# Retention and mixture of experts on one core: the second expert's rows prepared at later steps, weight splits moved into its pass, and one ordering between transfers dropped

## The chip, the cores and the metric

One core of a Trainium2 chip runs the whole kernel. Its engines are TensorE (PE, with its weight loads PEld), VectorE (DVE), ScalarE (ACT), GpSimd (POOL) and SyncE (SP, which only issues transfers here). The metric is device time in microseconds of one execution, given as the median of the runs shown. The granted clock of TensorE is a share of full speed: 1.0 is 2.4 GHz, 0.5 is 1.2 GHz.

## The reference, cut to what matters

```python
# attention with a decaying state, for each batch and head
for t in range(S):                                   # S = 768, head_dim 64, 8 heads, 4 batches
    state = gamma * state + outer(k[t], v[t])
    y[t] = scale * (q[t] @ state)
x = y as rows                                        # 3072 rows of 512
# one expert of 8 per row
e_idx = argmax(x @ w_gate, axis=1)
gate_w = softmax(x @ w_gate) at e_idx ;  eom = sigmoid(x @ w_output_gate)
for e in range(8):
    mask = e_idx == e
    h = maximum(x[mask] @ w1[e], 0)                  # 512 -> 1024
    out[mask] = gate_w * eom * (h @ w2[e])           # 1024 -> 512
```

## The kernel before, in words

The first part (to about 145 us) is the attention, in chunks; it also routes each row and scatters it by GpSimd into `srt`, a table in HBM that has 448 slots for each expert. Rows of empty slots are filled by three scatters of `zrow` (line L636): one with the indices `fi` for the first expert, two with the indices `si` for the rest. Nothing may read a slot before all of this is written; `after(ld.ins, sent)` says so for a load.

The second part multiplies the rows with the weights. Numbers are float32 split in a high and a low part, so each product is three matmuls: high by high, high by low, low by high. Experts are taken in an order of rank. The first expert is cut in two: its first 224 slots (`head`) run while the routing still ends; its last 224 (`left_load`, `left_turn`, `left_cast`, `left_sub`; tiles `xp`, `pt`, `ph`, `pw`) are pass e = 0 of the main loop. The seven other experts are passes 1 to 7, with 436 down to 364 slots.

The main loop runs over steps `s`, eight in a pass (`f` = 0 to 7), one for each block of 128 hidden units:

- `stage1(s)`: 12 matmuls (L1221) into one of three PSUM banks (`st`, and two named `h`), then `hh` on ScalarE (L1226, ReLU and rounding) and `hl` on VectorE (L1227, the rest).
- `stage2(s-1)`: 12 matmuls (L1241) that take `hh` and `hl` of the step before and add to the four accumulators `a`. At the end of a pass VectorE turns the accumulators (`ot`, L1247).
- `load_x(e)` loads the rows of an expert from `srt` (tile `xl`, four transfers on SyncE, L1188). That of pass 1 waits for all scatters.
- `prep_x(e, dc)` prepares one quarter of these rows: a transposition on VectorE (`xt`, L1207), a rounding on ScalarE (`xh`, L1208), a difference on VectorE (`xw`, L1209). The first quarter also takes the row numbers (`idi`, L1202), which is the first instruction that waits for `xl`.
- `load_weights(s)` loads a block of both weight matrices into one of three buffers `raw` (L158 and L162); `split_weights(s)` makes its high parts on ScalarE (`whi`, L184 and L186) and its low parts on VectorE (`wlo`, L191 and L193). The table in the `while split` line says how far the splits stay back at each step.

Each engine takes its instructions in the order in which they are written here; only SyncE's order in the second part is set by a scheduler. So an instruction of VectorE or ScalarE that waits holds up all that is written behind it. Block numbers below are values of `s`: block 10 is the third block of pass 1.

Of the kernel before, what the change touches and what calls it, by code (L numbers as in the profile page):

```python
# [32 lines left out]
def retention_moe_kernel(  # L33
# [17 lines left out]
    E, DM, DF = w1.shape  # L51
# [5 lines left out]
    NF = DF // P  # L57
# [10 lines left out]
    srt = dpool.tile([DROWS, ROW], F32, name="srt")  # L68
# [95 lines left out]
    def load_weights(s: int):  # L164
        for _ in weight_parts(s):
            pass
# [29 lines left out]
    def split_weights(s: int):  # L196
        for part in range(2):
            split_hi(s, part)
        for part in range(2):
            split_lo(s, part)  # L200
# [10 lines left out]
    def behind(later, earlier):  # L211
        tc.add_manual_dep(later, earlier.name, mybir.DependencyInfo(
            mybir.DependencyClass.Sync, mybir.DependencyReason.DATA), reason="one send at a time")
# [6 lines left out]
    with ExitStack() as actx:  # L220
# [28 lines left out]
        def after(ins, others):  # L249
            for o in others:  # L250
                tc.add_manual_dep(ins, o.name, mybir.DependencyInfo(
                    mybir.DependencyClass.Sync, mybir.DependencyReason.DATA), reason="sorted rows complete")
# [522 lines left out]
        def emit_head(n):  # L775
            return send(out.rearrange("t (a x) -> (t a) x", a=4), hd["idx"][:, n:n + 1], hd["ot"][:, n], 4 * NT)
# [171 lines left out]
        def left_load(eng, part):  # L948
            if part == 0:
                hd["p"] = wpool.tile([P, 8 * SEG], F32, name="xp", tag="raw", bufs=3)[:, 0:NL * SEG].rearrange("p (n x) -> p n x", x=SEG)  # L950
            t = hd["p"]
            for a in range(2 * part, 2 * part + 2):
                ld = eng.dma_start(
                    t[32 * a:32 * a + 32],
                    srt[ds(rank_e[0] * SLOTS + HEAD, LEFT), a * SEG:(a + 1) * SEG].rearrange("(n i) x -> i n x", i=32))
                if a % 2 == 0:
                    after(ld.ins, sent)

# [19 lines left out]
        def left_ids():  # L978
            hd["pm"] = hpool.tile([P, NL], I32, name="pm0")
            nc.vector.tensor_copy(hd["pm"], hd["p"][:, :, P])  # L980
            nc.vector.tensor_tensor(out=hd["pm"], in0=hd["pm"], in1=slot, op=ALU.max)
            return hd["pm"]
# [167 lines left out]
    with ExitStack() as mctx:  # L1150
# [26 lines left out]
        NS = E * NF  # L1177
# [5 lines left out]
        def load_x(e):  # L1183
            r0, n = PASS[e]
            nb = math.ceil(n / 32)
            t = mp.tile([P, NB, SEG], F32, name="xl", tag="xl")
            for a in range(4):
                ld = nc.sync.dma_start(  # L1188
                    t[32 * a:32 * a + 32, 0:nb],
                    srt[ds(r0, 32 * nb), a * SEG:(a + 1) * SEG].rearrange("(n i) x -> i n x", i=32))  # L1190
                if e == 1 and a == 0:
                    after(ld.ins, sent)
            xr[e] = t
# [17 lines left out]
        def stage1(s):  # L1211
            e, f = divmod(s, NF)
            hi, lo = wts[s]
            xh, xl = xs[e]
            C = PASS[e][1]
            ps = next_bank()
            n = 0
            first_of = (hi, xh), (lo, xh), (hi, xl)
            for dc, (l, r) in ([(dc, lr) for g in (0, 2) for lr in first_of for dc in (g, g + 1)] if e == 0
                               else [(dc, lr) for dc in range(NDC) for lr in ((hi, xh), (hi, xl), (lo, xh))]):  # L1220
                nc.tensor.matmul(ps[:, 0:C], l[:, 0, dc * P:dc * P + P], r[dc][:, 0:C] if e == 0 else r[:, dc, 0:C],  # L1221
                                 start=(n == 0), stop=(n == 3 * NDC - 1))
                n += 1
            hh = mp.tile([P, CAPS[0]], F32R, name="hh", tag="hh", bufs=3)[:, 0:C]
            hl = mp.tile([P, CAPS[0]], F32R, name="hl", tag="hl", bufs=3)[:, 0:C]
            relu = nc.scalar.activation(hh, ps[:, 0:C], AF.Relu)  # L1226
            nc.vector.scalar_tensor_tensor(out=hl, in0=ps[:, 0:C], scalar=0.0, in1=hh.bitcast(F32),  # L1227
                                           op0=ALU.max, op1=ALU.subtract)
            hs[s] = (hh, hl)
            return relu.ins  # L1230

        def stage2(s):
            e, f = divmod(s, NF)
            hi, lo = wts.pop(s)
            hh, hl = hs.pop(s)
            C = PASS[e][1]
            nb = math.ceil(C / 32)
            for d in range(4):
                w = slice(d * P, d * P + P)
                for n, (l, r) in enumerate(((hi, hh), (hi, hl), (lo, hh))):  # L1240
                    mm = nc.tensor.matmul(accs[d][:, 0:C], l[:, 1, w], r, start=(f == 0 and n == 0),  # L1241
                                          stop=(f == NF - 1 and n == 2))
            if f == NF - 1:

                ot = mp.tile([P, NB, P], F32, name="ot", tag="ot", bufs=2)
                for d in range(4):
                    nc.vector.transpose(ot[:, 0:nb, d * 32:d * 32 + 32],  # L1247
                                        accs[d][:, 0:32 * nb].rearrange("p (n i) -> p n i", i=32))
                ots[e] = ot
            return mm.ins  # L1250

        def emit(e, n):
            return send(out.rearrange("t (a x) -> (t a) x", a=4), xs["m", e][:, n:n + 1], ots[e][:, n], 4 * NT)

        def stage2_last(f, tb):
            hi, lo = wts[(E - 1) * NF + f]
            hh, hl = hs[(E - 1) * NF + f]
            w = slice(tb * P, min(tb * P + P, CAPS[-1]))
            n = w.stop - w.start
            for x, (l, r) in enumerate(((hh, hi), (hl, hi), (hh, lo))):  # L1260
                mm = nc.tensor.matmul(rows_of[tb][0:n], l[:, w], r[:, 1], start=(f == 0 and x == 0),
                                      stop=(f == NF - 1 and x == 2))
            return mm.ins

        def emit_last(tb):
            n = min(P, CAPS[-1] - tb * P)
            orow = mp.tile([P, DM], F32, name="orow", tag="orow", bufs=NTB)
            (nc.vector.tensor_copy if tb % 2 else nc.scalar.copy)(orow[0:n], rows_of[tb][0:n])
            send(out, idl[0:n, tb:tb + 1], orow[0:n], NT)
# [9 lines left out]
        loaded, split = NF + 2, NF  # L1279
        for s in range(NS + 1):  # L1280
            e, f = divmod(s, NF)
            if s == 1:
                load_x(1)
            while loaded < min(NS, s + NF + 1):
                load_weights(loaded)
                loaded += 1
            if f == 2 and 0 < e < E - 1:
                load_x(e + 1)
            if s < NS:
                relu = stage1(s)  # L1290
            if 1 <= s <= NS - NF:
                done = stage2(s - 1)
            elif s == NS:
                for tb in range(NTB):
                    stage2_last(NF - 2, tb)
                    stage2_last(NF - 1, tb)
                    emit_last(tb)
            elif s > 0 and s != NS - 2:
                for x in range(f - 1 if s < NS - 1 else NF - 3, min(f, NF - 2)):
                    for tb in range(NTB):  # L1300
                        done = stage2_last(x, tb)
            if s == 1:
                xs["m", 0] = left_ids()
            elif s == NF + 2:
                odd_rows()
            f0 = 3 if e == 0 else 4
            if f0 <= f < (f0 + 4 if e == 0 else 7) and e + 1 < E:
                for dc in (f - f0,) if e == 0 or f < 6 else (2, 3):
                    prep_x(e + 1, dc)
            while split < min(NS, s + NF - {3: 1, 4: 2, 5: 3, 6: 3, 7: 3, 8: 2, 9: 1}.get(s, 0)):  # L1310
                split_weights(split)
                split += 1
            if e >= 1 and s < NS and f >= 1:
                for n in range(2 * f - 2, min(math.ceil(PASS[e - 1][1] / 32), 2 * f)):
                    behind(emit(e - 1, n), done if n % 2 else relu)
            if e == 0:
                if f < HEAD // 32:
                    behind(emit_head(f), relu)
            if s == NS - NF:
                idl = load_idl(E - 1)  # L1320
# [4 lines left out]
    with tc.If(odd > 0):  # L1325
        with ExitStack() as octx:
# [72 lines left out]
            for r in range(1, E):  # L1399
                nov = nc.values_load(over[0:1, r - 1:r], min_val=0, max_val=SLOTS)  # L1400
                with tc.If(nov > 0):
                    e = nc.values_load(order[0:1, r - 1:r], engines=(mybir.EngineType.SP,), min_val=0, max_val=E - 1)
# [47 lines left out]
```

## Time and profile before

| | |
|---|---|
| median of 3 runs | 446.66 us (446.25 to 447.26) |
| the profiled execution, its own time | 444.65 us |
| its span in the trace | 442.9 us |
| TensorE busy | 409.9 us, 93% of the span |
| VectorE, ScalarE, GpSimd busy | 264.9, 199.3, 150.2 us |

The execution's own time is 1.75 us longer than its span: what lies before the first and behind the last instruction. A busy TensorE is not TensorE at its peak, since matmuls overlap and their ends are modelled; the start of a matmul is the safer number, and the text goes by starts.

### The profile page before, as it was taken

How to read it: one execution, taken by the hardware profiler on the slowest of the kernel's cores; microseconds unless marked ns; L12 is line 12 of the kernel's file. 1: busy time of each engine (PE TensorE's matmuls, PEld its weight loads, DVE VectorE, ACT ScalarE, POOL GpSimd, SP SyncE). 2: the span in 40 equal slices, each digit the busy share in tenths (PEclk: the TensorE clock that was granted, in tenths of full speed). 3: DMA queues.
4: the chain of work that ended last, by engine and by line, in shares of the span. 5: the costliest groups of instructions: out<-in, count | busy, mean ns of one | idle time of the engine just before them, and what ended most of it. 6: DMA issues, size and time to landing. Idle time of an engine off the chain costs nothing.

```text
span 442.9 us, 13007 instructions
## 1 busy us (share of the span) xinstructions
PE 409.9 (93%) x5080; PEld 389.5 (88%) x5082; DVE 264.9 (60%) x712; ACT 199.3 (45%) x411; POOL 150.2 (34%) x213
## 2 busy tenths in 40 slices
PE   7798998987989999799999999999999999999991
PEld 3677888976879898799999999999999999999881
DVE  2526777975887873576674565566466477475110
ACT  3334575773784822354443443353443354453110
POOL 7444022221223613213004443441542442441532
PEclk9989899998999999699999999999999999999997
DMA  9999999895551648359628437646745944940002
GB/s 181 206 222 231 212 268 221 211 262 161 172 141 54 233 140 198 119 172 255 211 95 210 159 126 178 180 125 188 211 125 158 231 139 151 228 142 14 30 26 72
DMA packets 125624, 73.74 MB, mean 166 GB/s; under 512 B 55845, under 2 KB 114105, under 8 KB 125552
## 3 DMA queue, kind: packets, MB, share of 16 engines
q1 hardware_dynamic: 119200, 59.07, 52.2%
q0 software_dynamic: 5872, 13.50, 9.2%
q8 instruction: 42, 0.69, 0.7%
q10 hardware_dynamic: 480, 0.23, 0.2%
q14 instruction: 30, 0.25, 0.2%
HBM read 59.63 MB, written 13.90 MB: 166 GB/s over the span
## 4 chain that ended last, share of the span: by engine, by line
PE 49%; issue 6%; POOL 3%; DMA 3%; DVE 1%; SPq 1%; POOLq 0%; ACT 0%; DVEq 0%
PE a L1241 24%; PE h L1221 17%; PE st L1221 8%; POOL out_dram L203 3%; DMA srt<-zrow,si 1%; DMA xl<-srt 1%; SPq L1188 1%; DVE pt L963 0%; POOLq L203 0%; DVE xw L1209 0%; ACT xh L1208 0%; DVE xt L1207 0%; POOLq L1135 0%; DVE hl L1227 0%; POOLq L1324 0%
## 5 line engine op out<-in xcount | busy, mean ns | idle before, releaser
L203 POOL DMA_INDIRECT out_dram<-ot,idi x77 | 78.6, 1021 | 138.9 <-ACT hh L1226 113.5
L1241 PE MATMUL a<-hh,whi 128*128 128x224 f32 (+6 forms) x224 | 75.8, 338 | 3.2 <-ACT hh L1226 3.2
L1241 PE MATMUL a<-hl,whi 128*128 128x224 f32 (+6 forms) x224 | 75.9, 339 | 0.1
L1241 PE MATMUL a<-hh,wlo 128*128 128x224 f32 (+6 forms) x224 | 75.7, 338 | 0.0
L191 DVE TENSOR_TENSOR wlo<-raw,whi 128x512 fp32r<-128x512 f32 x64 | 44.0, 687 | 34.5 <-ACT whi L184 32.9
L184 ACT CAST whi<-raw 128x512 fp32r<-128x512 f32 x64 | 39.5, 617 | 42.3 <-PE a L1241 37.7
L1221 PE MATMUL h<-xh,wlo 128*128 128x408 f32 (+6 forms) x148 | 50.6, 342 | 0.0
L1221 PE MATMUL h<-xw,whi 128*128 128x408 f32 (+6 forms) x148 | 50.6, 342 | 0.0
L1221 PE MATMUL h<-xh,whi 128*128 128x408 f32 (+6 forms) x148 | 50.6, 342 | 0.0
L636 POOL DMA_INDIRECT srt<-row,posi x20 | 20.2, 1012 | 77.5 <-ACT ex L481 11.7
L1241 PEld LDWEIGHTS a<-hh,whi 128*128 128x128 f32 x224 | 42.7, 191 | 3.7 <-ACT hh L1226 3.3
L1227 DVE SCALAR_TENSOR_TENSOR hl<-h,hh 128x224 fp32r<-128x224 f32 (+7 forms) x43 | 23.4, 544 | 37.0 <-ACT hh L1226 37.0
L193 DVE TENSOR_TENSOR wlo<-raw,whi 128x512 fp32r<-128x512 f32 x64 | 43.8, 684 | 0.0
L1241 PEld LDWEIGHTS a<-hl,whi 128*128 128x128 f32 x224 | 42.7, 191 | 0.8 <-DVE hl L1227 0.4
L1241 PEld LDWEIGHTS a<-hh,wlo 128*128 128x128 f32 x224 | 42.8, 191 | 0.4
L1226 ACT ACTIVATE hh<-h 128x224 fp32r<-128x224 f32 (+7 forms) x43 | 20.7, 481 | 49.8 <-PE h L1221 49.8
L368 PE MATMUL st<-vs,kn 64*64 64x64 f32 x704 | 34.4, 231 | 7.6 <-issue 3.9
L186 ACT CAST whi<-raw 128x512 fp32r<-128x512 f32 x64 | 39.4, 616 | 0.2
L368 PEld LDWEIGHTS st<-vs,kn 64*64 64x64 f32 x704 | 27.9, 141 | 6.9 <-ACT sx L428 2.2
L1208 ACT CAST xh<-xt 128x416 fp32r<-128x416 f32 (+2 forms) x28 | 14.9, 533 | 40.4 <-DVE xt L1207 40.4
L428 ACT COPY sx<-st 128x256 f32<-128x256 f32 x44 | 16.4, 373 | 32.9 <-PE st L368 31.7
L1221 PEld LDWEIGHTS h<-xh,whi 128*128 128x128 f32 x148 | 27.8, 188 | 0.4
(259 smaller groups left out, 889.6 us busy)
## 6 DMA issues: line engine op xcount, KB each, us to landing
raw<-in_moe_w_dram SPq DMA_DIRECT2D x128, 256.0 KB, 3.4
kn<-in_k_dram SPq DMA_DIRECT2D x24, 256.0 KB, 5.7
vn<-in_v_dram SPq DMA_DIRECT2D x24, 256.0 KB, 5.5
qn<-in_q_dram SPq DMA_DIRECT2D x14, 256.0 KB, 4.8
qn<-in_q_dram SPq DMA_DIRECT2D x5, 512.0 KB, 6.5
xl<-srt SPq DMA_DIRECT2D x12, 211.2 KB, 5.7
xl<-srt SPq DMA_DIRECT2D x12, 195.0 KB, 5.4
out_dram<-ot,idi POOLq DMA_INDIRECT x77, 3.0
```

Of the source, the lines that this page charges most:

```text
L184: nc.scalar.copy(hi[:, 0], raw[:, 0])
L186: nc.scalar.copy(perm(wts[s][0], s), plain(raw, s))
L191: eng.tensor_sub(lo[:, 0], raw[:, 0], hi[:, 0].bitcast(F32))
L193: eng.tensor_sub(perm(lo, s), plain(raw, s), perm(hi, s).bitcast(F32))
L203: st = nc.gpsimd.indirect_dma_start(out=dst, out_offset=bass.IndirectOffsetOnAxis(ap=idx, axis=0), in_=src, in_offset=None, bounds_check=n ...
L368: mm = nc.tensor.matmul(o, l, m, start=s, stop=True, skip_group_check=True)
L428: ins = nc.scalar.copy(t, st).ins
L636: ins = nc.gpsimd.indirect_dma_start(out=srt, out_offset=bass.IndirectOffsetOnAxis(ap=idx, axis=0), in_=src, in_offset=None, bounds_check= ...
L1221: nc.tensor.matmul(ps[:, 0:C], l[:, 0, dc * P:dc * P + P], r[dc][:, 0:C] if e == 0 else r[:, dc, 0:C], start=(n == 0), stop=(n == 3 * NDC ...
L1226: relu = nc.scalar.activation(hh, ps[:, 0:C], AF.Relu)
L1227: nc.vector.scalar_tensor_tensor(out=hl, in0=ps[:, 0:C], scalar=0.0, in1=hh.bitcast(F32), op0=ALU.max, op1=ALU.subtract)
L1241: mm = nc.tensor.matmul(accs[d][:, 0:C], l[:, 1, w], r, start=(f == 0 and n == 0), stop=(f == NF - 1 and n == 2))
```

## The change

Three edits, all around pass 0 and the first steps of pass 1:

- The four quarters of the second expert's rows, `prep_x(1, 0)` to `prep_x(1, 3)`, stood at steps 3, 4, 5 and 6. They now stand at step 5 (quarter 0), step 6 (quarters 1 and 2) and step 7 (quarter 3). For later passes the rule stays as it was.
- The table of splits holds back more at steps 6 to 10: blocks 10 and 11, which were split at steps 6 and 7, are split at step 8 with block 12; up to step 11 each step has its splits one block later.
- The load of the first expert's second half (`left_load`) joins the group of transfers on `srt` that need no order among themselves, so that the scatters of `zrow` into the other experts' empty slots no longer wait for it.

```diff
@@ left_load
                     srt[ds(rank_e[0] * SLOTS + HEAD, LEFT), a * SEG:(a + 1) * SEG].rearrange("(n i) x -> i n x", i=32))
+                tc.add_to_no_dep_group("srt", ld.ins)
                 if a % 2 == 0:
                     after(ld.ins, sent)
@@ main loop, step s = 8 * e + f
-            f0 = 3 if e == 0 else 4
-            if f0 <= f < (f0 + 4 if e == 0 else 7) and e + 1 < E:
-                for dc in (f - f0,) if e == 0 or f < 6 else (2, 3):
+            if (5 if e == 0 else 4) <= f < (8 if e == 0 else 7) and e + 1 < E:
+                for dc in ((0,), (1, 2), (3,))[f - 5] if e == 0 else (f - 4,) if f < 6 else (2, 3):
                     prep_x(e + 1, dc)
-            while split < min(NS, s + NF - {3: 1, 4: 2, 5: 3, 6: 3, 7: 3, 8: 2, 9: 1}.get(s, 0)):
+            while split < min(NS, s + NF - {3: 1, 4: 2, 5: 3, 6: 4, 7: 5, 8: 3, 9: 2, 10: 1}.get(s, 0)):
                 split_weights(split)
                 split += 1
```

On VectorE, in pass 0 from the `hl` of step 3 to the first `hl` of pass 1 (`hl<-st,hh 128x436`, step 8), the order before is:

```order
L1227 SCALAR_TENSOR_TENSOR hl<-h_3108,hh 128x224
L1202 CAST idi<-xl 128x14
L1207 STREAM_TRANSPOSE xt<-xl 128x448
L1209 TENSOR_TENSOR xw<-xt,xh 128x448
L1227 SCALAR_TENSOR_TENSOR hl<-h_3153,hh 128x224
...
L1227 SCALAR_TENSOR_TENSOR hl<-st,hh 128x224
...
L1227 SCALAR_TENSOR_TENSOR hl<-h_3108,hh 128x224
...
L191 TENSOR_TENSOR wlo<-raw,whi 128x512
L193 TENSOR_TENSOR wlo<-raw,whi 128x4x4x32
L1227 SCALAR_TENSOR_TENSOR hl<-h_3153,hh 128x224
```

and of the change, where lines between L957 and L1306 are numbered one higher:

```order
L1228 SCALAR_TENSOR_TENSOR hl<-h_3153,hh 128x224
L1228 SCALAR_TENSOR_TENSOR hl<-st,hh 128x224
L1203 CAST idi<-xl 128x14
L1208 STREAM_TRANSPOSE xt<-xl 128x448
L1210 TENSOR_TENSOR xw<-xt,xh 128x448
L1228 SCALAR_TENSOR_TENSOR hl<-h_3108,hh 128x224
...
L1228 SCALAR_TENSOR_TENSOR hl<-h_3153,hh 128x224
L1208 STREAM_TRANSPOSE xt<-xl 128x448
L1210 TENSOR_TENSOR xw<-xt,xh 128x448
L1228 SCALAR_TENSOR_TENSOR hl<-st,hh 128x436
```

The `hl` of steps 4 (`h_3153`) and 5 (`st`) moved ahead of `idi`; two quarters stand between the `hl` of steps 6 and 7, and the last one stands between those of steps 7 and 8. No split is left among them: those of blocks 10, 11 and 12 now follow the four `ot` behind the `hl` of step 8. ScalarE's `hh` and `xh` moved in the same way.

On GpSimd, the last scatter of rows (`bposi`), the two scatters of `zrow` by `si`, and the read of `n_pad`, by which it branches past further such scatters, before (the names in brackets are counters: DMAHW of SyncE's and ScalarE's transfers, DMASW of GpSimd's, the others of engines):

```order
L636 DMA srt<-row,bposi 6784x520 [waits Activation_49]
L636 DMA srt<-zrow,si 6784x520 [waits DMAHW6_49,DMAHW5_49,DMAHW7_49,DMAHW0_49,DVE_49]
L636 DMA srt<-zrow,si 6784x520 [waits DMASW3_49,DVE_49]
L1135 TENSOR_LOAD n_pad [waits DVE_49]
L1135 ISA x2
L1136 COMPARE_AND_BRANCH
```

and of the change:

```order
L636 DMA srt<-row,bposi 6784x520 [waits Activation_49]
L636 DMA srt<-zrow,si 6784x520 [waits DVE_49]
L636 DMA srt<-zrow,si 6784x520 [waits DMASW3_49,DVE_49]
L1136 TENSOR_LOAD n_pad [waits DVE_49]
L1136 ISA x2
L1137 COMPARE_AND_BRANCH
```

The first scatter lost its four waits for the transfers of `left_load` and keeps the one for its indices; the rest stands as it stood.

On SyncE, behind the weights of block 17, the rows of the change read as follows; before, the read of `n_odd` (a count that VectorE makes at step 10) stood four blocks of weights behind the `xl` of pass 2:

```order
L1324 TENSOR_LOAD n_odd
L1324 ISA x2
L158 ISA
L158 DMA raw<-in_moe_w_dram 128x4x128
L162 ISA
L162 DMA raw<-in_moe_w_dram 128x512
L1189 ISA
L1189 DMA xl<-srt 32x13x130
```

So the weights of block 18 and the rows of pass 2 now stand behind a wait for VectorE's `n_odd`.

## Rows read from the trace of the kernel before

**Rows 1.** The page: granted clock in 40 slices, in tenths.

```profile
PEclk9989899998999999699999999999999999999997
```

**Rows 2.** Timeline of TensorE, steps 3 to 10: start, length, engine, line, operation, [idle before].

```profile
169.25 0.39 PE L1221 MATMUL h<-ph,whi 128*128 128x224 f32 x2
...
174.62 0.39 PE L1221 MATMUL st<-ph,whi 128*128 128x224 f32 x2
...
179.27 0.55 PE L1241 MATMUL a<-hh,whi 128*128 128x224 f32 x1 [3.16 <-ACT hh L1226]
...
188.97 0.37 PE L1221 MATMUL st<-xh,whi 128*128 128x436 f32 x1
...
190.75 0.35 PE L1221 MATMUL st<-xh,whi 128*128 128x436 f32 x1
...
192.67 0.37 PE L1221 MATMUL h<-xh,whi 128*128 128x436 f32 x1
...
197.43 0.36 PE L1221 MATMUL h<-xh,whi 128*128 128x436 f32 x1
```

**Rows 3.** Windows: stretch, length, busy of five engines, PEclk, DMA share, GB/s.

```profile
176.12:179.27 3.15, 0.00 (x0) 0.00 (x0) 1.00 (x3) 0.82 (x2) 0.00 (x0) 0.80 1.11 362
179.27:184.96 5.69, 5.54 (x25) 5.27 (x25) 3.31 (x7) 1.39 (x3) 1.94 (x2) 0.51 0.27 89
```

**Rows 4.** The chain that ended last, 155 to 190 us: start, length, what.

```profile
162.71 6.15 DMA srt<-zrow,si
...
171.81 5.64 DMA xl<-srt
```

**Rows 5.** Timeline of VectorE, 158 to 212 us.

```profile
158.42 0.16 DVE L1125 TENSOR_TENSOR si<-sl,pidx 128x1 int32<-128x1 f32 x1
...
171.21 0.38 DVE L1227 SCALAR_TENSOR_TENSOR hl<-h,hh 128x224 fp32r<-128x224 f32 x1
177.64 0.18 DVE L1202 CAST idi<-xl 128x14 int32<-128x14 f32 x1 [6.05 <-DMA xl<-srt]
177.72 0.64 DVE L1207 STREAM_TRANSPOSE xt<-xl 128x448 f32<-128x448 f32 x1
178.99 0.62 DVE L1209 TENSOR_TENSOR xw<-xt,xh 128x448 fp32r<-128x448 f32 x1 [0.63 <-ACT xh L1208]
179.54 0.38 DVE L1227 SCALAR_TENSOR_TENSOR hl<-h,hh 128x224 fp32r<-128x224 f32 x1
179.84 0.64 DVE L1207 STREAM_TRANSPOSE xt<-xl 128x448 f32<-128x448 f32 x1
...
211.48 0.17 DVE L1202 CAST idi<-xl 128x13 int32<-128x13 f32 x1 [0.77 <-DMA xl<-srt]
```

**Rows 6.** Timeline of ScalarE, 170 to 179 us.

```profile
170.79 0.36 ACT L1226 ACTIVATE hh<-h 128x224 fp32r<-128x224 f32 x1 [0.31 <-PE h L1221]
178.40 0.56 ACT L1208 CAST xh<-xt 128x448 fp32r<-128x448 f32 x1 [7.25 <-DVE xt L1207]
178.87 0.35 ACT L1226 ACTIVATE hh<-h 128x224 fp32r<-128x224 f32 x1
```

**Rows 7.** Timeline of GpSimd: the first scatter of `zrow` by `si`.

```profile
161.43 0.97 POOL L636 DMA_INDIRECT srt<-zrow,si  x1 [7.30 <-DVEq L1136]
```

**Rows 8.** Timeline of SyncE: the issues of weights of block 9, of `xl` of pass 2.

```profile
163.77 0.52 SPq L162 DMA_DIRECT2D raw<-in_moe_w_dram  x1
...
201.28 2.26 SPq L1188 DMA_DIRECT2D xl<-srt  x4
```

**Rows 9.** Tile `raw`, 188 to 216 us: last line.

```profile
DMA to landing us min/median/max: 2.9/4.5/8.2
```

**Rows 10.** Tile `xl`, 200 to 216 us: last line.

```profile
DMA to landing us min/median/max: 5.4/6.8/8.2
```

**Rows 11.** The page, costliest groups: busy us, mean ns of one | idle before.

```profile
L191 DVE TENSOR_TENSOR wlo<-raw,whi 128x512 fp32r<-128x512 f32 x64 | 44.0, 687 | 34.5 <-ACT whi L184 32.9
...
L1227 DVE SCALAR_TENSOR_TENSOR hl<-h,hh 128x224 fp32r<-128x224 f32 (+7 forms) x43 | 23.4, 544 | 37.0 <-ACT hh L1226 37.0
```

## The prediction

> **What bounds it now.** I read the page first. TensorE is busy for nearly all of the second part, and among its slices of granted clock one stands out after the attention: a 6 in a row of nines, around 180 us [rows 1]. The timeline of TensorE there shows why. Step 5 of pass 0 begins at 174.62, and its `stage2` should follow 12 matmuls later; it begins at 179.27, after 3.16 us idle for `hh` [rows 2]. Behind the wait the matmuls are slow: the windows show the clock at 0.80 in the idle stretch and 0.51 in the next 5.69 us, so nearly all of that stretch is at 1.2 GHz [rows 3].
>
> Then I asked why `hh` of step 4 was late. On ScalarE it stands behind `xh` of the second expert's first quarter, and starts right after it, at 178.87 [rows 6]. `xh` waited 7.25 us for `xt`, and VectorE, which makes `xt`, sat 6.05 us before `idi` until the transfer `xl` landed [rows 5, 6]. The chain of waits carries this further back: `xl` was held by the second scatter of `zrow`, 6.15 us from its start at 162.71 until SyncE was released, and the last of its four transfers took 5.64 us from 171.81, so it landed at 177.45 [rows 4]. So for one quarter of rows that nobody needs before step 8, two engines kept in order hold back what TensorE needs at step 5. From step 8 to the end TensorE runs step after step, so what is saved here should move the end by as much.
>
> **What the wait costs.** Steps of pass 0 with nothing in the way take (174.62 − 169.25) / 2 = 2.685 us [rows 2]. From 174.62 three of them would bring step 8 to 182.68; it begins at 188.97 [rows 2]. The loss is 6.29 us. Two parts make it up: the first matmul of `stage2` comes 3.31 us after 174.62 + 1.34 = 175.96, and the 24 matmuls of the stretch from 179.27 to 184.96 take 5.69 us where 2.685 is the rate at full clock, 3.00 us more [rows 2, 3].
>
> The Trainium skill (TensorE: Matmul & The Clock Gate, Terms) puts the penalty of a lowered clock at the time spent low times (1 − K/N), here a half. The low time, an estimate from the windows, is (1 − 0.80)/0.5 × 3.15 + (1 − 0.51)/0.5 × 5.69 = 6.8 us [rows 3], which by that rule is 3.4 us and would make the loss 6.7. The rows say 3.0, since for the first 1.3 us of the low time TensorE had nothing to run; the sum goes by the rows.
>
> **Edit 1: the rows taken up later.** Nothing is added: four `xt`, `xh` and `xw` move. I follow the new order with durations of before. `hh` starts 170.79 − 169.25 = 1.54 us after its step, and `hl` 0.42 after `hh` [rows 2, 5, 6]. So `hl` of step 5 starts at 174.62 + 1.54 + 0.42 = 176.58 and frees VectorE 0.30 later (179.54 to 179.84 [rows 5]), at 176.88. If `xl` is there, `idi` follows, and no `hh` or `hl` of steps 4 and 5 waits for it: the loss of 6.29 us goes.
>
> What is late next: the quarters. One of them takes VectorE 1.82 us from the start of `xt` to its next instruction (177.72 to 179.54), because `xw` waits for ScalarE [rows 5]. Step 6 begins at 174.62 + 2.685 = 177.30, its `hl` at 179.26, so quarter 1 begins at 179.56, quarter 2 at 181.38, `hl` of step 7 at 183.20 and quarter 3 at 183.50. Its `xh` starts 0.68 later and takes 0.56 [rows 5, 6], so it ends at 184.74; its `xw` starts 1.27 later, takes 0.62 [rows 5], and ends at 185.39. TensorE wants quarter 3 with the tenth matmul of step 8, 190.75 − 188.97 = 1.78 us into it [rows 2], at 182.68 + 1.78 = 184.46. It waits some 0.33 us for `xh`, and one matmul (0.20) later another 0.40 for `xw`: **0.75 us lost**. Quarters 0 to 2 are in time by this reckoning. Bounds: 0 if VectorE and ScalarE run half a step ahead of this, 1.05 if `xl` lands as late as now (next paragraph).
>
> **Edit 3: the scatters no longer held.** The first `si` is ready at 158.42 + 0.16 = 158.58 [rows 5], and the scatter starts at 161.43 [rows 7]. Waiting for VectorE alone, it starts between at once and 0.97 us later (the length of one scatter [rows 7]); so the pair moves forward by 1.9 to 2.85 us. SyncE is free for it: its last issue ahead of `xl` is that of block 9, at 163.77 for 0.52 [rows 8]. With the same 6.15 and 5.64 us behind it, `xl` lands at 174.6 to 175.55, ahead of the 176.88 at which VectorE now asks for it. Beside edit 1 this is worth little: at 177.45 `idi` would start at 177.64 and `xt` at 177.72, against 176.96, which delays `hl` of step 6 from 179.26 to 179.54 [rows 5] and everything behind it by 0.28. **Worth 0.3 us**, already in the 0.75; the lower bound is 0, the upper, with edit 1 undone, the 1.9 to 2.85 us by which `idi` would come earlier.
>
> **Edit 2: splits moved.** The same casts and subtractions are issued, and the splits of blocks 10 and 11 leave the place where they would have stood between the `hl` of steps 6 and 8. Blocks 10, 11 and 12 are split behind `ot` of step 8. Step 8 starts at 182.68, takes 192.67 − 188.97 = 3.70 us and loses 0.75, so step 9 starts at 187.13 and step 10, 197.43 − 192.67 = 4.76 later, at 191.89 [rows 2]. Block 10 is needed at step 10 and ready near 190: no wait. But a `raw` buffer is free only when its block is split, so loads of block 13 on start later against TensorE than before. Step 13 starts at 187.13 + 4 × 4.76 = 206.17 and its `hl` is not yet asked for; step 14's `stage2` asks for it at 206.17 + 4.76 + 2.4 + 0.2 = 213.5. Ahead of it on VectorE stand `idi`, quarter 0 of pass 2 and the split of block 19 (two `wlo` of 0.6 to 0.7 [rows 11]). Now `xl` of pass 2 is issued at 201.28 and `idi` starts at 211.48 [rows 5, 8]. Its issue follows block 18, for which the split of block 15 must be done; by the same reckoning that is near 200.4, so the issue stays where it is while TensorE comes 5.5 us earlier. If the landing stays too, `hl` ends at 211.48 + 1.9 + 1.3 + 0.5 = 215.2 and TensorE waits **1.7 us**. If its transfers land in the 5.4 us of the fastest and not in 6.8 to 8.2 [rows 10], `idi` starts near 209 and the wait is **0**. Fewer weights are queued ahead of it (blocks 16 and 17 are asked for about a microsecond earlier), so I take 0.6, nearer to the fast end. The wait for `n_odd` now ahead of block 18 on SyncE costs nothing: VectorE makes `n_odd` before the split of block 15, for which block 18 waits anyway.
>
> **The sum.** 6.29 − 0.75 − 0.6 = 4.9 us. On its own time the profiled execution would come to 444.65 − 4.9 = 439.7; that execution is 2.0 below the median of the runs, and the same 4.9 off the median gives 441.7.
>
> **The rivals.**
>
> *A, the half clock comes back at step 8.* The waits of 0.33 and 0.40 us are short, and the clock fell here behind one of 3.16 [rows 2, 3]. But other small waits stand close by, and if it falls once more, it costs up to the 3.0 us measured for the 24 matmuls: 441.7 to 444.7, say 443.8. Chance 0.13.
>
> *B, the rows of pass 2 come late.* The `hl` of step 13 is late by the whole 1.7 us, as above: 442.4. If one more step is late by as much, because its weights need the 8.2 us of the slowest load and not the median 4.5 [rows 9], it is 6.29 − 0.75 − 3.4 = 2.1, so 444.5. Chance 0.14.
>
> *C, slower: the three `raw` buffers turn into the bound.* Block 14 is asked for near 191.7; with 8.2 us [rows 9], then its high part (0.6, as a `xh`), its second low part (0.69 [rows 11]) and `hl` of step 10 (0.54 [rows 11]) `stage2` could start at 201.7, against 191.89 + 4.76 + 2.6 = 199.25, some 2.5 us late. Each third block waits for the one before, so blocks 14, 17 and 20 would lose 7.5: 446.66 − 5.5 + 7.5 = 448.7. It decides once the three lose more than 5.5 together. Against it: the median is 4.5, at which block 14 leaves a cushion of more than a microsecond. Chance 0.05.
>
> *D, no change:* the wait of step 5 is for something else and stays, or is given back in full. 446.7. The chain names each link, so 0.06.
>
> **How the numbers follow.** The forecast, 440.4 to 442.8 (both new waits at 0, 440.4; both at their upper ends, 1.05 and 1.7, 443.1), has 0.62. The spread of the runs, 446.25 to 447.26, adds half a microsecond at the low end: 439.8. At the high end the range takes in A and most of B: 444.7. What lies outside is C, D and the rest of B, under 2 in 10. About 0.2% (0.9 us) is what a measurement of this kernel tells from no change: faster 0.88, same 0.07, slower 0.05.
>
> **What would show it.** In the profile of the changed kernel: no wait over 1 us on TensorE between 162 us and its end, no 6 among the slices near 180; the first scatter by `si` at 158.9 to 159.5; `idi` of pass 1 right behind `hl` of step 5, without a wait for `xl`; two short waits near 184.5 at the tenth and eleventh matmul of step 8, and step 9 at 187.1; a wait of 0 to 1.7 us in step 14. It is wrong if the clock is low again between 178 and 190, if `idi` still waits for `xl`, or if ScalarE's `whi` waits for `raw` hold `hh` in steps 10 to 14.

## The result and the profile after

| | before | after |
|---|---|---|
| median of 9 runs each | 446.25 us (443.31 to 447.26) | 440.89 us (438.42 to 443.90) |
| span of the profiled execution | 442.9 us | 439.3 us |
| its first matmul of pass 0 | 162.24 us | 162.50 us |
| from the start of step 5 to that of step 16 | 51.32 us | 47.51 us |

The ratio is 0.9893 (0.9859 to 0.9928): 4.8 us faster, 3.2 to 6.3 by the interval, with 4.9 forecast. Here and below a ratio is taken from the fast runs alone (none over 1.5% above the fastest of its kernel) and a median from all runs, so a ratio is not the quotient of two medians. The two traces differ by 3.6 us in span, and all of it arises between step 5 and step 16 (3.81 us; pass 0 begins 0.26 later, and from step 16 to the end it is 216.99 and 216.92 us).

The page after: span, and the granted clock in 40 slices. The 6 of [rows 1] is gone.

```profile
span 439.3 us, 13006 instructions
PEclk9899899998999999999999999999999999999997
```

TensorE after, as in [rows 2], steps 5, 8, 9, 14 and 15 by their first matmuls, and the matmuls that waited:

```profile
174.87 0.39 PE L1222 MATMUL st<-ph,whi 128*128 128x224 f32 x2
...
182.91 0.37 PE L1222 MATMUL st<-xh,whi 128*128 128x436 f32 x1
...
184.49 0.36 PE L1222 MATMUL st<-xh,wlo 128*128 128x436 f32 x1
185.06 0.47 PE L1222 MATMUL st<-xh,whi 128*128 128x436 f32 x1 [0.21 <-ACT xh L1209]
185.72 0.47 PE L1222 MATMUL st<-xw,whi 128*128 128x436 f32 x1 [0.19 <-DVE xw L1210]
...
187.57 0.37 PE L1222 MATMUL h<-xh,whi 128*128 128x436 f32 x1
...
211.29 0.36 PE L1222 MATMUL st<-xh,whi 128*128 128x436 f32 x1
...
214.45 0.46 PE L1242 MATMUL a<-hh,whi 128*128 128x436 f32 x1 [0.64 <-ACT hh L1227]
215.35 0.46 PE L1242 MATMUL a<-hl,whi 128*128 128x436 f32 x1 [0.44 <-DVE hl L1228]
...
217.63 0.36 PE L1222 MATMUL h<-xh,whi 128*128 128x436 f32 x1
```

Steps 5 to 7 take 8.04 us together where they took 14.35 [rows 2], so 6.3 us came back there. Some is given away again at two later places. Step 8 takes 4.66 us and 3.70 before: 0.96 lost, at its tenth and eleventh matmul. Step 14 takes 6.34 us where steps 9 to 13 take 4.75 each: 1.59 lost.

The windows of steps 5 to 7, step 8, steps 9 to 13 and step 14 (busy time of TensorE, weight load, VectorE, ScalarE, GpSimd, then granted clock, DMA share, GB/s):

```profile
174.87:182.91 8.04, 8.04 (x75) 8.04 (x73) 3.78 (x8) 2.43 (x6) 2.41 (x3) 1.00 0.51 167
182.91:187.57 4.66, 4.26 (x27) 3.51 (x25) 2.62 (x5) 1.89 (x5) 0.00 (x0) 1.00 0.00 0
187.57:211.29 23.72, 23.72 (x123) 22.52 (x121) 15.93 (x37) 11.63 (x21) 7.10 (x7) 1.00 0.78 212
211.29:217.63 6.34, 5.26 (x25) 4.42 (x24) 4.76 (x10) 3.80 (x8) 0.00 (x0) 1.00 0.77 235
```

The clock stays at 1.00 through all four, the two waits included. Note the zeros of the second: in step 8 no transfer runs at all, because the three `raw` buffers are full and wait for their splits; in the next 23.72 us the queues work at 0.78.

VectorE after, as in [rows 5]:

```profile
176.80 0.39 DVE L1228 SCALAR_TENSOR_TENSOR hl<-st,hh 128x224 fp32r<-128x224 f32 x1 [2.29 <-ACT hh L1227]
177.11 0.16 DVE L1203 CAST idi<-xl 128x14 int32<-128x14 f32 x1
...
183.47 0.39 DVE L1228 SCALAR_TENSOR_TENSOR hl<-h,hh 128x224 fp32r<-128x224 f32 x1
183.78 0.64 DVE L1208 STREAM_TRANSPOSE xt<-xl 128x448 f32<-128x448 f32 x1
185.04 0.63 DVE L1210 TENSOR_TENSOR xw<-xt,xh 128x448 fp32r<-128x448 f32 x1 [0.63 <-ACT xh L1209]
...
211.66 0.17 DVE L1203 CAST idi<-xl 128x13 int32<-128x13 f32 x1 [4.31 <-DMA xl<-srt]
...
214.69 0.60 DVE L1228 SCALAR_TENSOR_TENSOR hl<-h,hh 128x436 fp32r<-128x436 f32 x1
```

In pass 0 `idi` follows the `hl` of step 5 without a wait. In step 14 `idi` of pass 2 waits 4.31 us for its rows, and `hl` of step 13 stands behind it. The chain of waits between the two lost places (start, duration, what):

```profile
190.66 0.61 DVE wlo L193
191.30 0.38 SPq L158
...
191.88 5.03 DMA raw<-in_moe_w_dram
196.93 0.63 ACT whi L186
197.58 0.69 DVE wlo L193
...
200.80 0.70 DVE wlo L193
201.52 0.38 SPq L158
...
204.57 7.06 DMA xl<-srt
211.66 0.17 DVE idi L1203
```

and the issue of the rows of pass 2 on SyncE:

```profile
202.63 2.26 SPq L1189 DMA_DIRECT2D xl<-srt  x4
```

Read backwards: the rows of pass 2 were issued behind block 18, that waited for the split of block 15, that stood behind the split of block 14, and block 14 could only be asked for at 191.30, when the splits held back to step 8 had freed a buffer. The two scatters of `zrow` by `si`, as in [rows 7]:

```profile
159.09 0.97 POOL L636 DMA_INDIRECT srt<-zrow,si  x1 [4.71 <-DVE sc L1124]
160.37 0.97 POOL L636 DMA_INDIRECT srt<-zrow,si  x1 [0.31 <-issue]
```

Against the start of pass 0 the first one moved from 0.81 us ahead to 3.41 ahead, 2.6 us earlier.

### The profile page after: what moved, and what is told of

The parts are those of the page before. It is cut to its first block, busy times and chain, and to the rows that moved or that the text cites. A ratio compares the mean times of both kernels' runs of the same rounds, so it can differ in the third digit from the quotient of the medians.

```text
span 439.3 us, 13006 instructions
## 1 busy us (share of the span) xinstructions
PE 408.3 (93%) x5082; PEld 387.1 (88%) x5082; DVE 264.7 (60%) x712; ACT 199.4 (45%) x411; POOL 150.2 (34%) x213
## 4 chain that ended last, share of the span: by engine, by line
PE 44%; issue 6%; POOL 3%; DVE 3%; DMA 3%; ACT 1%; SPq 1%; POOLq 0%; DVEq 0%; ACTq 0%
PE a L1242 22%; PE h L1222 15%; PE st L1222 7%; POOL out_dram L203 3%; DMA xl<-srt 2%; DMA raw<-in_moe_w_dram 1%; DVE wlo L193 1%; DVE hl L1228 1%; DVE xt L1208 1%; DVE xw L1210 0%; ACT xh L1209 0%; SPq L1189 0%; DVE wlo L191 0%; ACT hh L1227 0%; DVE ot L1248 0%
```

## The experiments

Two theories were set against each other. The prediction's (R in the expectations): the place of the quarters decides, so edit 1 (rows later) carries the gain, edit 2 (splits) spares step 8, and edit 3 (scatters not held) adds 0.3. The rival (T): the landing decides, so edit 3 alone removes the wait, and edits 1 and 2 only move it.

What stands in front of pass 0 takes a different time in each execution: pass 0 began between 160.46 and 168.34 us over the 13 traces, and the five with the whole change (e5, e6 and e7 build on it), which are the same program up to there, span 161.84 to 166.26. So the kernels are compared first by the time from the start of step 5 to that of step 16 in their traces. With nothing late it would be 3 × 2.685 + 3.70 + 7 × 4.75 = 45.0 us; what is above that is lost. From step 16 to the end all 13 traces agree within 0.7 us (216.92 to 217.58). Kernels e1 to e4 ran in one batch, e5, e6, e7 and e9 in a second, both on the chip recorded as number 12, and the last three in a third, on number 4. Each ratio is to runs of the kernel before in the same batch; their medians were 444.48, 448.94 and 448.39 us. Kernels that ran once have no ratio, and only their traces are used.

| kernel | edits | median us (runs) | ratio to before | steps 5 to 15, us | lost | lost at |
|---|---|---|---|---|---|---|
| before | none | 446.25 (9) | | 51.32 | 6.3 | step 5, 6 |
| after | 1, 2, 3 | 440.89 (9) | 0.9893 (0.9859 to 0.9928) | 47.51 | 2.5 | 8, 14 |
| e1_no_hold | 3 | 437.18 (6) | 0.9857 (0.9796 to 0.9917) | 45.11 | 0.1 | 5 |
| e2_rows_late | 1 | 440.19 (12) | 0.9939 (0.9903 to 0.9976) | 48.74 | 3.7 | 8, 9 |
| e3_rows_no_hold | 1, 3 | 439.50 (6) | 0.9887 (0.9821 to 0.9954) | 48.75 | 3.7 | 8, 9 |
| e4_rows_splits | 1, 2 | 438.95 (12) | 0.9908 (0.9873 to 0.9942) | 47.05 | 2.0 | 8, 14 |
| e5_quarters | all, quarters by twos | 443.05 (1), before 448.94 | | 45.66 | 0.7 | 14 |
| e6_xl_early | all, `load_x(2)` earlier | 444.79 (1), before 448.94 | | 47.59 | 2.6 | 8, 13 |
| e9_splits_only | 2 | 445.79 (1), before 448.94 | | 51.94 | 6.9 | 5, 6, 14 |
| e7_both | e5 and e6 | 442.27 (6) | 0.9843 (0.9800 to 0.9886) | 46.10 | 1.1 | 13 |
| e1_again | 3 | 444.52 (6) | 0.9880 (0.9809 to 0.9950) | 45.29 | 0.3 | 5 |
| after_again | 1, 2, 3 | 442.67 (6) | 0.9894 (0.9839 to 0.9948) | 46.39 | 1.4 | 8, 14 |
| e10_splits_no_hold | 2, 3 | 446.41 (1), before 448.39 | | 46.71 | 1.7 | 5, 14 |

### Edit 3 alone

```diff
@@ left_load, against the kernel before
+                tc.add_to_no_dep_group("srt", ld.ins)
```

> Edit 3 alone: the old order of rows and splits, but the scatters are not held. Theory R (the gain is that of the rows taken up later): the rows of pass 1 land 2 to 3 us earlier, but VectorE and ScalarE still stand before them at steps 3 and 4, so the wait of TensorE in step 5 shrinks only to about 1 us or more; the gain is 2 to 3 us, well under that of the whole change. Theory T (the gain is that of the earlier transfer): the rows land near 174.7, the quarter is done when stage2 of step 5 is due, the wait is under 1 us and the clock stays up; 6.3 - 0.8 = 5.5 us, as much as the whole change or more, since nothing is lost at steps 8 and 14.

It lost 0.1 us where the kernel before lost 6.3. SyncE's waits before and with edit 3 alone (engine and line, what for, us in total, times, longest) show what the hold was:

```profile
SPq L1188 <- DMA srt<-zrow,si: 4.5, 1, 4.5
```

```profile
SPq L1189 <- DMA srt<-zrow,si: 0.2, 1, 0.2
```

Its timeline: the second scatter on GpSimd and the issue of `xl` on SyncE,

```profile
158.51 0.97 POOL L636 DMA_INDIRECT srt<-zrow,si  x1 [0.31 <-issue]
```

```profile
163.24 1.92 SPq L1189 DMA_DIRECT2D xl<-srt  x4
```

then VectorE, ScalarE and TensorE around step 5, which begins at 172.99:

```profile
172.11 0.17 DVE L1203 CAST idi<-xl 128x14 int32<-128x14 f32 x1 [2.14 <-DMA xl<-srt]
...
174.01 0.38 DVE L1228 SCALAR_TENSOR_TENSOR hl<-h,hh 128x224 fp32r<-128x224 f32 x1
```

```profile
173.34 0.35 ACT L1227 ACTIVATE hh<-h 128x224 fp32r<-128x224 f32 x1
```

```profile
174.33 0.27 PE L1242 MATMUL a<-hh,whi 128*128 128x224 f32 x1
174.45 0.37 PE L1242 MATMUL a<-hl,whi 128*128 128x224 f32 x1
174.66 0.28 PE L1242 MATMUL a<-hh,wlo 128*128 128x224 f32 x1
```

`idi` still waits, 2.14 us, and `hh` of step 4 still stands behind `xh`. But `stage2` of step 5 is due 1.34 us after 172.99, at 174.33, and starts then; only `hl` costs it 0.10. Against the start of pass 0 (160.62) `idi` comes 11.49 us later; before it was 15.40 later, so 3.9 us were won, more than the 3.31 that TensorE waited. With no wait left on TensorE the clock stayed at 1.00 (steps 5 to 7, 172.99 to 181.13), and the 3.00 us of half clock went with it. So theory T's expectation is met, and that of R (a wait of 1 us or more left) is not.

The 3.9 us are more than the 2.6 by which the scatter starts earlier, since the scatter is also shorter: it lands 3.0 us after its start, and 4.9 in the kernel before. In these stretches the transfer queues were busy for a share of 0.38 and 0.83; before, the scatter runs beside the weights of blocks 8 and 9, issued from 161.77 to 163.77, and now mostly ahead of them. That this overlap makes it longer is likely, and no run here tests it alone.

### Edit 1 alone, edits 1 and 3, edits 1 and 2

```diff
@@ main loop, against the kernel before (edit 1; e3_rows_no_hold adds the line of edit 3, e4_rows_splits the table of edit 2)
-            f0 = 3 if e == 0 else 4
-            if f0 <= f < (f0 + 4 if e == 0 else 7) and e + 1 < E:
-                for dc in (f - f0,) if e == 0 or f < 6 else (2, 3):
+            if (5 if e == 0 else 4) <= f < (8 if e == 0 else 7) and e + 1 < E:
+                for dc in ((0,), (1, 2), (3,))[f - 5] if e == 0 else (f - 4,) if f < 6 else (2, 3):
```

> Edit 1 alone: rows at steps 5 to 7, old table of splits, scatters held. Theory R: the wait of step 5 and the half clock are gone; blocks 10 and 11 are now split between the quarters, which makes the last quarter 1.2 us later, so step 8 loses about 2.3 us, step 14 nothing; gain near 4 us. Theory T: without the earlier landing the rows come at 177.5 and the gain is small, under 2 us.

> Edits 1 and 3 without the table of splits (edit 2 undone). Both theories: step 5 does not wait. If edit 2 is what keeps step 8 short, step 8 loses about 2.1 us here and not 0.96, and step 14 loses 0 and not 1.6, since the loads of block 13 on start earlier; together 2.1 against 2.6 us, so the time is that of the whole change within 1 us.

> Edits 1 and 2, scatters held (edit 3 undone). Theory R: 0.3 us slower than the whole change, all of it at step 8 (1.2 to 1.3 us lost there and not 0.96). Theory T: most of the gain is gone.

With edit 1 alone steps 5 to 7 take 2.68 us each: this edit too removes the wait of step 5, although `xl` is as late as before (`idi` comes 15.19 us behind the start of pass 0 and still waits for it, as the first line below on VectorE shows). But much of the loss comes back at step 8. TensorE there, the ninth to eleventh matmul of step 8 and the first of step 9:

```profile
182.46 0.36 PE L1221 MATMUL st<-xh,wlo 128*128 128x436 f32 x1
184.27 0.46 PE L1221 MATMUL st<-xh,whi 128*128 128x436 f32 x1 [1.45 <-ACT xh L1208]
184.93 0.47 PE L1221 MATMUL st<-xw,whi 128*128 128x436 f32 x1 [0.20 <-DVE xw L1209]
...
187.15 0.59 PE L1221 MATMUL h<-xh,whi 128*128 128x436 f32 x1
```

VectorE ahead of it, where the split of block 10 stands between the third quarter and the `hl` of step 7:

```profile
175.65 0.33 DVE L1202 CAST idi<-xl 128x14 int32<-128x14 f32 x1 [0.49 <-DMA xl<-srt]
...
181.47 0.69 DVE L191 TENSOR_TENSOR wlo<-raw,whi 128x512 fp32r<-128x512 f32 x1
182.08 0.69 DVE L193 TENSOR_TENSOR wlo<-raw,whi 128x512 fp32r<-128x512 f32 x1
182.68 0.39 DVE L1227 SCALAR_TENSOR_TENSOR hl<-h,hh 128x224 fp32r<-128x224 f32 x1
182.98 0.64 DVE L1207 STREAM_TRANSPOSE xt<-xl 128x448 f32<-128x448 f32 x1
```

and the window behind it:

```profile
186.33:189.74 3.41, 3.41 (x14) 3.19 (x13) 3.41 (x8) 1.96 (x4) 0.00 (x0) 0.50 0.49 159
```

The two `wlo` put 1.2 us in front of the last quarter; the tenth matmul comes 1.81 us after the ninth instead of 0.20, the eleventh 0.66 after the tenth instead of 0.20. That is 2.07 us, and then the clock is at 0.50, its level of 1.2 GHz, for 3.41 us. Steps 8 and 9 take 12.23 us for 8.45, so 3.78 are lost, and 1.71 of them fall to the clock. The Trainium skill (TensorE: Matmul & The Clock Gate, Terms) gives 3.41 × (1 − 1/2) = 1.7 for it; the trace agrees, as TensorE had work in all of this stretch. Theory R had expected the lateness (2.3 us); the clock was in neither theory.

Edit 3 on top (e3_rows_no_hold) changes nothing: 48.75 against 48.74 us, and the 2.1 us of loss that was expected became 3.7, as the half clock came back here too. Edit 2 on top (e4_rows_splits) takes 1.7 us of the loss away: step 8 takes 4.77 us, at full clock. But step 14 now takes 5.74. So edit 2 repairs most of what edit 1 does to step 8, and step 14 pays. Beside edits 1 and 2, edit 3 takes 0.11 us off step 8 (4.77 without it, 4.66 with it), where theory R had expected 0.3.

### Edit 2 alone, and edits 2 and 3

```diff
@@ main loop, against the kernel before (e10_splits_no_hold adds the line of edit 3)
-            while split < min(NS, s + NF - {3: 1, 4: 2, 5: 3, 6: 3, 7: 3, 8: 2, 9: 1}.get(s, 0)):
+            while split < min(NS, s + NF - {3: 1, 4: 2, 5: 3, 6: 4, 7: 5, 8: 3, 9: 2, 10: 1}.get(s, 0)):
```

> Edit 2 alone (the old place of the rows, scatters held). Both theories: the wait of step 5 and the half clock stay, 6.3 us lost at steps 5 and 6; nothing is gained. Theory that later splits cost by themselves: with TensorE 6 us later the loads of block 13 on are in time, so step 14 loses 0 and the time is that of the kernel before within 0.5 us.

> Edits 2 and 3, rows at their old place. If the later splits are the cause at step 14, steps 5 and 8 lose 0 to 0.2 us as with edit 3 alone and step 14 loses 0.5 to 1.6. If the place of the rows is the cause, step 14 takes its 4.75 us.

Both lose at step 14, 0.57 and 1.32 us (5.32 and 6.07 for 4.75), with the quarters where they were before; no kernel without edit 2 loses there. So step 14 is the price of edit 2. For edit 2 alone this is a miss: no loss was expected there, since TensorE is not earlier than in the kernel before, and the rows of pass 2 are late all the same.

How it comes about shows in the distance from the issue of pass 2's `xl` to the start of step 14: 15.2 us before and 15.1 with edit 3 alone, 8.7 after, 9.0 and 9.1 in the two kernels of this section. The splits held back to step 8 hold the three buffers; in step 8 of edit 3 alone the queues carry 154 GB/s, where after shows zeros:

```profile
181.13:184.83 3.70, 3.70 (x26) 3.58 (x25) 2.50 (x5) 2.02 (x5) 0.00 (x0) 1.00 0.52 154
```

An idle stretch of the queues is not enough by itself: with edit 1 alone they carry 41 GB/s in the first 3.70 us of step 8, but the issue stays 16.2 us ahead of step 14 and nothing is lost there.

That the landing of these rows sets the loss can be read from all six traces that have edit 2 and the rows asked for at step 10. In order of the landing, `idi` starts 0.79, 0.67, 0.63 and 0.23 us ahead of the start of step 14 (after_again, e9, e5, e4) and 0.08 and 0.37 behind it (e10, after); the step loses 0.45, 0.57, 0.59, 0.99, 1.32 and 1.59. Each time the loss is 1.2 us more than the lateness of `idi`.

### Two repairs of the whole change

```diff
@@ e5_quarters, against the changed kernel
-                for dc in ((0,), (1, 2), (3,))[f - 5] if e == 0 else (f - 4,) if f < 6 else (2, 3):
+                for dc in ((0, 1), (2, 3), ())[f - 5] if e == 0 else (f - 4,) if f < 6 else (2, 3):
@@ e6_xl_early, against the changed kernel
-            if f == 2 and 0 < e < E - 1:
+            if f == (0 if e == 1 else 2) and 0 < e < E - 1:
```

> The whole change, but quarters 0 and 1 of the rows of pass 1 at step 5, 2 and 3 at step 6. If the loss at step 8 is the chain of the quarters on VectorE and ScalarE: quarter 3 then ends 1.0 us earlier, step 8 takes 3.7 to 3.8 us and not 4.66. If something else holds step 8 (the bank, the weights of block 8), it stays at 4.66. Step 14 loses 1 to 1.6 us as before this edit.

> The whole change, but the rows of pass 2 are asked for at step 8 and not at step 10, ahead of the weights of blocks 17 and 18. If the loss at step 14 is the late landing of these rows: step 14 takes 4.75 to 5.0 us and not 6.34. If it is the weights of block 19, which both engines also wait for there, at least 1 us of the loss stays. Step 8 keeps its 0.9 to 1.1.

> The whole change with both mends (two quarters a step from step 5, rows of pass 2 asked for at step 8). If steps 8 and 14 are the only places where the change gives something back, the lost time falls from 2.55 us to 0.2 and the gain on the kernel before from 3.7 to 6.1 us, a ratio near 0.986. If the mends only move the waits, less than 4.5 us is gained.

Two quarters at step 5 and two at step 6, none behind the `hl` of step 7, bring step 8 to 3.82 us: 0.1 is left of the loss there. This shows that the last quarter's place was its cause. Step 14 loses 0.6, less than the 1 to 1.6 expected.

The earlier load of the rows did not help. With it step 13 takes 6.34 us and step 14 4.79: the wait moved one step ahead and kept its size. ScalarE in step 13:

```profile
209.56 0.62 ACT L184 CAST whi<-raw 128x512 fp32r<-128x512 f32 x1 [4.52 <-DMA raw<-in_moe_w_dram]
...
212.77 0.53 ACT L1227 ACTIVATE hh<-h 128x436 fp32r<-128x436 f32 x1
```

Now the weights that were ahead of the rows stand behind them, and `hh` stands behind a `whi` that waits for these weights. Step 14 is as short as the first expectation had it, and yet nothing is won. So it is not the place of one load: after a step without transfers, the weights and the rows of pass 2 all have to come before step 14, and in each order that was run one of them is late. Both edits together (e7_both) lose 1.1 us, 1.0 of it at step 13, where 0.2 in all was expected.

### Edit 3 alone against the whole change, on one chip

> Edit 3 alone, a second time, beside the whole change on the same chip. If edit 3 alone is worth the whole wait (steps 5 to 15 lost 0.1 us in the first trace, against 6.3 before and 2.5 with the whole change), it is 6 us faster than before and 2 to 2.5 us faster than the whole change. If its first time owed something to that chip, the two are alike within 1 us.

> The whole change on the same chip as edit 3 alone: 3.5 to 5 us faster than before, 2 to 2.5 us slower than edit 3 alone. Its trace loses about 1 us at step 8 and 1 to 1.6 us at step 14 again.

From step 5 to step 15 edit 3 alone lost 0.3 us and the whole change 1.4. The timed runs don't show the 2 to 2.5 us between them that were expected, and don't tell them apart: 440.82 to 447.93 us with edit 3 alone, 439.39 to 445.30 with the whole change. In this trace edit 3 alone entered pass 0 at 167.45 us and the whole change at 161.84, which outweighs the difference; the first trace of the same kernel entered at 160.62. Why the time in front of pass 0 varies so is open.

## Why the prediction was right, and where it was not

**The bound and its price: right.** The wait of step 5 and the half clock behind it were on the path; step 8 begins 8.04 us after step 5, by the prediction's sum 8.06. The loss of 6.29 us went in full. The total was met more closely than the terms were: the runs say 4.8 us (3.2 to 6.3) for a forecast of 4.9, while the first trace of the change gained 3.8 on that of before and the second 4.9. That the median came within 0.1 us is luck.

**Edit 1, the last quarter: right in place, a little small.** Two short waits, at the tenth and eleventh matmul of step 8, were forecast with 0.33 and 0.40. The two matmuls came 0.37 and 0.46 late; the whole step lost 0.96, for 0.75 forecast and a bound of 1.05.

**Edit 2, the rows of pass 2: a term mis-sized.** The step "fewer weights are queued ahead of it [...], so I take 0.6, nearer to the fast end" failed in the first trace: 1.59 us, near the bound of 1.7, so half of rival B. The issue did not stay at 201.28 but came at 202.63, since the split of block 15 ended a microsecond later than reckoned (at 201.50, for 200.4), and `idi` waited until 211.66. The size varies: 1.59 and 0.45 in the two traces of this program, 0.99 with edits 1 and 2. In both traces of this program the issue lies 8.7 us ahead of step 14, and `idi` follows it after 9.03 and 7.94 us; this difference in landing makes the difference in loss. The mean of the two, 1.0, is above the 0.6 taken. The reason given was half right: the prediction let the issue stay where it was while TensorE came earlier, but with edit 2 alone TensorE came no earlier, and the issue was as close to step 14 and the rows were late. The splits moved the issue.

**Edit 3: the attribution failed.** The prediction gave it 0.3 us beside edit 1, and with edit 1 undone 1.9 to 2.85. Beside edit 1 it is worth nothing that can be seen (48.74 and 48.75), beside edits 1 and 2 0.11 at step 8; alone it is worth 6.2 and 6.0 us between steps 5 and 16 in its two traces. Two things were wrong in the figure for edit 3 alone. The scatter moved by 2.6 us, as reckoned, but the 6.15 us from its start to SyncE's release were taken as fixed, and with edit 3 they are at most 4.73 (158.51 to 163.24), so `idi` came 3.9 us earlier. And the 2.85 was treated as a gain of its own size, though a wait of 3.31 us that shrinks to nothing takes the half clock with it: past that point the 3.00 us come on top. So each of the two edits removes the same 6.3 us, and together they can't remove it twice. That the total came out right rests on the loss that both remove, not on the reckoning of which edit does it.

**Rivals.** A: no return of the clock in the whole change, but it returned in both kernels with edit 1 and without edit 2; edit 2 is what kept it away. C and D: no sign; the load of block 14 took 5.03 us of the 8.2 that C needed. The extra wait for `n_odd` ahead of block 18 cost nothing, as said: the chain goes through the split of block 15. One sum of rival B is off: with the whole 1.7 us lost, 6.29 − 0.75 − 1.7 = 3.84 is left and the time is 442.8, not 442.4; this is still inside the range.

**Open.** Whether edit 3 alone is faster in time than the whole change: from step 5 to step 15 it loses 1.1 to 2.4 us less, but the spread of what stands in front of pass 0 covers that. Whether the weights beside it are what makes the second scatter land after 4.9 us instead of 3.0. A fourth `raw` buffer, which would free the loads in step 8, was not tried.

## What to carry to other kernels

Where a late arrival blocks an engine that works in order, look first at what holds the transfer itself: one dropped ordering gave 6.0 to 6.2 of the 6.3 us of this stage with nothing to pay behind it, while moving the work to later steps gave it back in part at the next two places that needed the engine or the buffers. A wait that starts a stretch of half clock is worth its length only until it is gone, and then the clock's loss on top. When edits remove the same wait, run each alone before giving one of them the gain, and compare by the stage they touch when another stage varies by more.

## What the runs showed of the hardware

- The same program (edit 3 alone) entered pass 0 at 160.62 us in one trace and at 167.45 in another, on different chips; the median of the kernel before moved from 444.48 to 448.94 us between two batches on one chip number. From step 16 to the end all traces agreed within 0.7 us.
- A first matmul 1.6 us late, and a next one 0.46 late, were followed by 3.41 us at 1.2 GHz (edit 1 alone). In the whole change 0.37 and 0.46 us at step 8, and 0.80 and 0.70 at step 14, left the clock at 2.4 GHz. The stretch at 1.2 GHz was not longer behind a longer wait: in the kernel before TensorE was idle for 3.16 us and some 6.8 us were low, with edit 2 alone it was idle for 3.88 us and 3.4 were (181.6 to 185.0 us).
- The same scatter of `zrow` landed 4.9 us after its start and released SyncE after 6.15 when it started 0.47 us behind the start of pass 0 (queues at 0.83), and landed after 3.0 and released SyncE after at most 4.73 when it started 2.11 ahead of it (queues at 0.38).
